# Two attention blocks on one core: A's x and first query weights are loaded from ScalarE's queue

## The chip, the cores and the metric

The kernel runs on one core of a Trainium2 chip. TensorE multiplies matrices, VectorE and ScalarE work elementwise, GpSimd does small set-up work, and SyncE (SP) computes nothing: it issues loads and stores. All loads and stores are carried out by 16 DMA engines. The metric is the device time of one launch in microseconds (us); lower is better.

## The reference

Two independent attention blocks with a key and value cache are computed, and their outputs are set side by side. All data is bf16; the batch is 16, there are 32 queries for each batch element and a cache of 1024 keys, heads have 128 elements, and the model width is 1024.

```python
q = (x @ wq).reshape(B, Sq, 32, 128).transpose(0, 2, 1, 3)
scores = einsum("bhqd,bhkd->bhqk", q, k) * 128 ** -0.5
o = einsum("bhqk,bhkd->bhqd", softmax(scores), v)
out = o.transpose(0, 2, 1, 3).reshape(B, Sq, 32 * 128) @ wo
```

Block A has 4 key and value heads that 8 query heads share each; block B has 32 key and value heads. The caches of B are 128 MB each and those of A 16 MB each, and the kernel reads every byte once, about 338 million bytes in all.

## The kernel before

The kernel streams the caches through SBUF and interleaves A's and B's work. In the code the index `pi` is 0 for A and 1 for B. B's K tiles go through 8 buffers (`KB_sb`), its V tiles through 6 (`VB_sb`), A's through two of each (`KA_sb`, `VA_sb`). A step computes scores on TensorE, the row maximum on VectorE (L1038), the exponential on ScalarE (L1051), transposes of the probabilities on TensorE, and the product with V on TensorE (L1083 for A, L1116 for B). B's K is transposed in place on VectorE (L976), A's on TensorE (L969). The output projection (L823) follows each group.

The first 40 us are a prologue. `xT_stage` (L655) loads x in four pieces of 0.25 MB for each block (L659; `x1_0` to `x1_3` for B, `x0_0` to `x0_3` for A), transposes each piece with eight TensorE transposes (L671), and copies the result to `xT_sb` on ScalarE or VectorE (L651). The pieces 1 to 3 of a block are declared to read what its piece 0 writes, so their issue waits for piece 0 to land. `wq_load` (L707) loads query weights in four pieces of 0.5 MB (L714): `wq0` to `wq3` into `wq_sb`, except for A's first part, which goes into `woA_sb` as `wqA0` to `wqA3`. Then TensorE projects the queries, L754 for B and L735 for A.

The program is not emitted in the order in which it is written. Each operation is recorded with an engine, what it reads and writes, and, for a load, a semaphore key (`dma_key`). `list_schedule` (L249) simulates all engines with the durations of a table, gives each operation a start time `t0`, and chooses ScalarE or VectorE for operations that either can do. The operations are then sorted by `t0` into one list (L494) and recorded again, which derives the dependences and waits anew. `emit_all` (L507) gives each engine its own operations in the order of that list. So the order on an engine is fixed when the program is built, and an instruction that waits holds back everything behind it on its engine.

All loads are recorded for SP. They are issued in list order into one queue: `x1_0`, `x0_0`, `wq0` to `wq3`, `wqA0`, A's first K tile, `x1_1` to `x1_3`, `x0_1` to `x0_3`, `wqA1` to `wqA3`, and then B's K and V tiles and the rest. Seven of the eight output rows that are stored from `acc` go through GpSimd's queue (L847).

Of the kernel before, what the change touches and what calls it, by code (L numbers as in the profile page):

```python
# [23 lines left out]
WQ_DELAY = 1  # L24
A_STEPS_FRAC = 0.96
SP_STRICT = False
SP_AHEAD = 5
DMA_MARGIN = {"kb_dma": 0.5, "vb_dma": 0.5, "ka_dma": 0.5, "va_dma": 0.5}
DMA_MARGIN_DEFAULT = 2.0
# [88 lines left out]
def actual(res):  # L118
    out = []
    for r in res:  # L120
        if not isinstance(r, Virt):
            out.append(r)
        else:
            out.append((r.cls, r.idx))
    return tuple(out)


class Prog:
# [120 lines left out]
    def list_schedule(self, lat=0.05, look=LOOK):  # L249
        ops = self.ops  # L250
        n = len(ops)
# [133 lines left out]
        order = []  # L385
# [34 lines left out]
        while True:  # L420
# [7 lines left out]
            for eng, lst in ready.items():  # L428
# [3 lines left out]
                if eng == "sp":  # L432
                    fe = max(fe, dma_free[0] - SP_AHEAD)
                if eng == "dve":
# [17 lines left out]
                key = (st, end, -bl[ci])  # L452
# [12 lines left out]
            if beng == "sp":  # L465
                st = max(st, dma_free[0] - SP_AHEAD)
            if beng == "pe":
# [23 lines left out]
                if ndeps[u] == 0:  # L491
                    make_ready(u)
        assert len(order) == n, "cycle in dependency graph?"
        seq = sorted(range(n), key=lambda k: (ops[order[k]].t0, k))  # L494
        newp = Prog()
        for k in seq:
            eng, emit, reads, writes, dma_key, name, dur, tag, prio = self.specs[order[k]]
            if eng == "any":
                eng = chosen[order[k]]
                name = name + "@" + eng  # L500
            newp.add(eng, emit, actual(reads), actual(writes), dma_key, name, dur, tag, prio)
        return newp

# [899 lines left out]
```

## Time and profile before

| What | Value |
|---|---|
| median of 3 runs | 850.99 us (847.71 to 854.19) |
| the profiled execution | 851.34 us, its span 849.5 us |
| granted TensorE clock, mean | 0.995 |
| TensorE busy | 783.0 us (92%) |
| VectorE busy | 727.0 us (86%) |
| ScalarE busy | 623.6 us (73%) |
| SP's queue | 337.95 million bytes |
| DMA rate over the span | 402 GB/s |

The span is the part of an execution that the profile covers, from the first instruction to the last. Busy times are sums over the span and not over stages: an engine with 92% can still be the one that everything waits for in one stage and idle in another. In the page's slices a digit is the busy share in tenths, and 9 means 90% or more. L numbers are lines of the kernel before.

### The profile page before, as it was taken

Reading aid. Unit: us, or ns where it says so; the run is one execution under the profiler, and the core shown is the slowest. Engines: PE = TensorE matmul, PEld = TensorE weight load, DVE = VectorE, ACT = ScalarE, POOL = GpSimd, SP = SyncE. Lnnn points to the kernel's source line nnn. Section 1 sums busy time; section 2 is a strip of 40 time slices with the busy share of each in tenths; the row PEclk is TensorE's granted clock in tenths of the full one; section 3 lists DMA queues with packets and bytes.
Section 4 is the critical chain, followed back from the end, with each engine's and each line's share of the span. In section 5 each row is a group of like instructions: output and inputs, shape, how many; then the busy total and the mean of one; then the engine's idle time right before and its main releaser. Section 6 shows DMA issues by size and latency. Waiting matters only on the chain.

```text
span 849.5 us, 29749 instructions
## 1 busy us (share of the span) xinstructions
PE 783.0 (92%) x13056; PEld 522.6 (62%) x13056; DVE 727.0 (86%) x1018; ACT 623.6 (73%) x1363; POOL 6.1 (1%) x20
## 2 busy tenths in 40 slices
PE   7989999999898999998999988999899998899878
PEld 4456665666565566665666665666666666666655
DVE  1499987979799898987999898998999978998995
ACT  3497787778677777786788787677877867686874
POOL 1000000000000000000000000000000000000000
PEclk9999999999999999999999999999999999999999
DMA  9999999999999999999999999999999999999995
GB/s 339 415 412 414 411 411 410 405 393 394 416 384 412 409 395 415 416 398 412 414 392 408 411 392 416 415 416 405 410 402 415 412 414 415 415 400 414 416 418 226
DMA packets 112208, 341.68 MB, mean 402 GB/s; under 512 B 12048, under 2 KB 12304, under 8 KB 112080
## 3 DMA queue, kind: packets, MB, share of 16 engines
q1 hardware_dynamic: 111520, 337.95, 100.0%
q8 instruction: 103, 1.69, 0.7%
q0 software_dynamic: 560, 1.84, 0.5%
q14 instruction: 25, 0.20, 0.1%
HBM read 337.64 MB, written 2.10 MB: 400 GB/s over the span
## 4 chain that ended last, share of the span: by engine, by line
PE 55%; DVE 23%; ACT 14%; DMA 5%; issue 2%; SPq 1%; DVEq 0%; ACTq 0%
DVE stat L1038 10%; PE psum L1116 10%; PE psum L823 10%; DVE KB_sb L976 8%; ACT P_sb L1051 8%; PE psum L1027 6%; PE psum L1063 5%; PE psum L754 5%; PE psum L1097 5%; PE psum L1083 4%; DMA KB_sb<-in_B_k_cache_dram 4%; PE psum L995 4%; PE psum L735 4%; ACT PT_sb L651 2%; ACT O_sb L1174 1%
## 5 line engine op out<-in xcount | busy, mean ns | idle before, releaser
L1038 DVE TENSOR_REDUCE stat<-psum 128x1 f32<-128x1024 f32 x256 | 303.6, 1210 | 50.7 <-PE psum L995 31.5
L1051 ACT ACTIVATE P_sb<-psum,stat 128x1024 bf16<-128x1024 f32 x246 | 275.9, 1122 | 63.2 <-DVE stat L1038 59.7
L976 DVE STREAM_TRANSPOSE KB_sb<-KB_sb 128x1024 f32<-128x1024 f32 x240 | 286.6, 1222 | 6.2 <-DMA KB_sb<-in_B_k_cache_dram 6.0
L651 ACT COPY PT_sb<-psum 128x512 f32<-128x512 f32 x226 | 131.4, 604 | 35.2 <-PE psum L1063 22.0
L1116 PE MATMUL psum<-VB_sb,PT_sb 64*64 64x256 bf16 x3584 | 116.2, 271 | 8.6 <-ACT P_sb L1051 5.2
L1116 PEld LDWEIGHTS psum<-VB_sb,PT_sb 64*64 64x64 bf16 x3584 | 97.0, 107 | 27.7 <-issue 25.5
L1174 ACT ACTIVATE O_sb<-psum,stat 128x128 bf16<-128x128 f32 (+1 forms) x205 | 80.8, 417 | 43.2 <-PE psum L1083 23.1
L1063 PE MATMUL psum<-id,P_sb 128*128 128x128 f32 x512 | 88.7, 297 | 6.9 <-ACT P_sb L1051 4.1
L1063 PEld LDWEIGHTS psum<-id,P_sb 128*128 128x128 f32 x512 | 74.0, 208 | 25.2 <-ACT P_sb L1051 13.8
L995 PE MATMUL psum<-KTA_sb,QT_sb 128*128 128x512 bf16 x256 | 84.4, 384 | 3.1 <-ACT P_sb L1051 1.6
L1083 PE MATMUL psum<-VA_sb,PT_sb 128*128 128x128 bf16 x1024 | 78.8, 221 | 7.5 <-ACT P_sb L1051 2.6
L1083 PEld LDWEIGHTS psum<-VA_sb,PT_sb 128*128 128x128 bf16 x1024 | 63.2, 99 | 31.6 <-issue 12.0
L1027 PE MATMUL psum<-KB_sb,QR 32*32 32x512 bf16 x3840 | 73.3, 394 | 8.1 <-ACT P_sb L1051 4.6
L1097 PE MATMUL psum<-id,P_sb 128*128 128x128 f32 x472 | 76.2, 287 | 4.1 <-ACT P_sb L1051 3.5
L754 PE MATMUL psum<-wq_sb,xT_sb 128*128 128x512 bf16 x256 | 72.4, 394 | 3.3 <-DMA wq_sb<-in_B_wq_dram 1.6
L1097 PEld LDWEIGHTS psum<-id,P_sb 128*128 128x128 f32 x472 | 63.8, 193 | 17.3 <-ACT P_sb L1051 7.5
L823 PE MATMUL psum<-woB_sb,OTB_sb 128*128 128x512 bf16 x256 | 66.9, 380 | 2.4 <-ACT P_sb L1051 1.7
L1027 PEld LDWEIGHTS psum<-KB_sb,QR 32*32 32x32 bf16 x3840 | 43.8, 89 | 35.3 <-ACT P_sb L1051 8.3
L823 PE MATMUL psum<-woA_sb,OTA_sb 128*128 128x512 bf16 x256 | 62.8, 380 | 0.4 <-ACT OTA_sb L651 0.3
L735 PE MATMUL psum<-xT_sb,wq_sb 128*128 128x512 bf16 x192 | 54.2, 380 | 1.7 <-issue 1.2
L1051 ACT ACTIVATION_READ_ACCUMULATOR P_sb<-psum,stat 128x1 f32 x246 | 50.3, 205 | 0.0
L835 DVE TENSOR_TENSOR acc<-acc,psum 128x512 f32<-128x512 f32 x64 | 41.3, 675 | 9.6 <-PE psum L823 9.4
(74 smaller groups left out, 720.2 us busy)
## 6 DMA issues: line engine op xcount, KB each, us to landing
KB_sb<-in_B_k_cache_dram SPq DMA_DIRECT2D x240, 512.0 KB, 8.9
VB_sb<-in_B_v_cache_dram SPq DMA_DIRECT2D x234, 512.0 KB, 7.8
KA_sb<-in_A_k_cache_dram SPq DMA_DIRECT2D x64, 256.0 KB, 7.8
VA_sb<-in_A_v_cache_dram SPq DMA_DIRECT2D x64, 256.0 KB, 8.0
wq_sb<-in_B_wq_dram SPq DMA_DIRECT2D x16, 512.0 KB, 8.3
woB_sb<-in_B_wo_dram SPq DMA_DIRECT2D x32, 256.0 KB, 8.5
woA_sb<-in_A_wo_dram SPq DMA_DIRECT2D x32, 256.0 KB, 7.0
wq_sb<-in_B_k_cache_dram SPq DMA_DIRECT2D x16, 512.0 KB, 11.5
```

The costliest lines, as they stand in the source:

```text
L651: return e.copy(dst, src) if hasattr(e, "activation") else e.tensor_copy(dst, src)
L754: last = e.matmul(bank(v)[:, 0:CW], xT_sb[:, 1, j, G * P:(G + 1) * P], wq_sb[:, j, mh * CW:(mh + 1) * CW], start=(j == 0), stop=(j == DJ - 1))
L823: last = e.matmul(bank(v)[:, 0:OUTW], OT[:, gp, hh, :], wo_[:, hh, oh * OUTW:(oh + 1) * OUTW], start=(hh == 0), stop=(hh == nh - 1))
L976: pr.add("dve", lambda e: e.transpose(tile_k(x).bitcast(F32), tile_k(x).bitcast(F32)), writes=[home_k(x)], name="KBt_tr", rtag={home_k(x): ...
L995: pr.add("pe", lambda e, u=u: e.matmul(bank(vS[u]), qt[:, q.b, q.hh0:q.hh0 + 4, :].rearrange("p a q -> p (a q)"), KTA_sb[:, sl, u * 512:(u ...
L1027: last = e.matmul(bank(q.vS[g2])[32 * x:32 * x + 32, :].rearrange("p (s j) -> p s j", s=16), lhsT, rhs, start=(fp == 0), stop=(fp == 3), t ...
L1038: pr.add("dve", lambda e: e.tensor_reduce(stat[:, vst.idx, 0:1], both(vS), AXIS.XY, ALU.max, negate=True), writes=vS + [vst], name="max")
L1051: return e.activation(dst, src, ACTF.Exp, bias=stat[:, vst.idx, 0:1], scale=1.0, accum_out=stat[:, vst.idx, 1:2])
L1063: last = e.transpose(bank(vb)[:, m * P:(m + 1) * P], p32[:, m:Sk // 2:NPK], id32[:])
L1083: last = e.matmul(bank(vb)[:, 0:Dh], ptc_of(vPT, c, 0, P), VA_sb[:, kvs, c, :], start=(c == 0), stop=(c == NCH - 1))
L1097: last = e.transpose(bank(vb)[:, m * P:(m + 1) * P], p32[:, 4 * h + m:Sk:8], id32[:])
L1116: last = e.matmul(bank(q.vbo)[n0:n0 + 64, 0:2 * Dh].rearrange("p (i d) -> p i d", i=2), pt2_chunk(vPT, c, e0, n0), v2[e0:e0 + 64, :, c, :] ...
```

## The change

Loads whose key starts with `x0` or `wqA` are sorted to the front of the list and recorded for ScalarE instead of SP. There are eight: `x0_0` to `x0_3` and `wqA0` to `wqA3`, 3.0 MB in all. Among themselves they keep the order of the list: `x0_0`, `wqA0`, `x0_1` to `x0_3`, `wqA1` to `wqA3`. ScalarE issues them ahead of its first copy, into its own queue. All other operations keep their engine and their order. The schedule itself is not simulated anew.

```diff
+ON_ACT = ('x0', 'wqA')
...
-        seq = sorted(range(n), key=lambda k: (ops[order[k]].t0, k))
+        seq = sorted(range(n), key=lambda k: (-1.0 if str(ops[order[k]].dma_key).startswith(ON_ACT) else ops[order[k]].t0, k))
         newp = Prog()
         for k in seq:
             eng, emit, reads, writes, dma_key, name, dur, tag, prio = self.specs[order[k]]
             if eng == "any":
                 eng = chosen[order[k]]
                 name = name + "@" + eng
+            if dma_key is not None and dma_key.startswith(ON_ACT):
+                eng = "act"
             newp.add(eng, emit, actual(reads), actual(writes), dma_key, name, dur, tag, prio)
```

## The prediction, made before the result was known

> **What bounds the kernel now.** I read the page first, then the start of the timeline, the chain of work, the tables by stage, and last the landings of single loads. (MB is 1024 x 1024 bytes here; x1 and wq are B's x and query weights, x0 and wqA are A's.) The page gives the chain by engine and the DMA engines' load:
>
> ```profile
> PE 55%; DVE 23%; ACT 14%; DMA 5%; issue 2%; SPq 1%; DVEq 0%; ACTq 0%
> DMA  9999999999999999999999999999999999999995
> ```
>
> The reader is to see two limits lying on each other: the DMA engines are full to the last slice, and yet the chain that ends last runs nearly all of its length through computing. The stages tell which one gives way:
>
> ```profile
> 4.00:6.00 2.00, 1.54 (x15) 1.28 (x13) 0.00 (x0) 1.28 (x2) 0.00 (x0) 1.00 0.89 220
> 190.00:200.00 10.00, 9.86 (x143) 5.96 (x139) 9.68 (x11) 8.77 (x19) 0.00 (x0) 1.00 0.98 359
> ```
>
> The last number is GB/s. Most stages have 400 to 418; 190 to 200 has 359, 240 to 250 has 354, 430 to 440 has 373. There the loads had run short because buffers came free late, so computing sets the pace at those points. In return, data is late to the engines by only 1.0 us in all after 50 us (VectorE's waits for KB loads, 0.2, 0.5 and 0.3 us). So a shift of all computing in the first 40 us should reach the end nearly whole, and the question is what the change does to those 40 us.
>
> The timeline of the start (start, duration, engine, line):
>
> ```profile
> 0.74 1.28 ACT L651 ACT_TABLE_LOAD   x1 [0.74 <-PEq L1388]
> 0.74 0.38 SPq L659 DMA_DIRECT2D acc<-in_B_x_dram  x1
> 1.17 0.42 SPq L659 DMA_DIRECT2D acc<-in_A_x_dram  x1
> 1.65 1.96 SPq L714 DMA_DIRECT2D wq_sb<-in_B_wq_dram  x4
> 4.72 1.93 ACT L651 COPY xT_sb<-psum 128x1024 bf16<-128x1024 bf16 x2 [2.70 <-PE psum L671]
> 7.61 1.43 SPq L659 DMA_DIRECT2D acc<-in_A_x_dram  x3
> 9.08 1.46 SPq L714 DMA_DIRECT2D woA_sb<-in_A_wq_dram  x3
> ```
>
> and the chain there and at its next DMA link:
>
> ```profile
> 1.65 5.44 DMA wq_sb<-in_B_wq_dram
> 7.13 5.79 PE psum L754 x14
> 18.93 6.22 PE psum L735 x28
> 25.51 12.86 DMA KB_sb<-in_B_k_cache_dram
> ...
> 198.67 10.08 DMA KB_sb<-in_B_k_cache_dram
> ```
>
> TensorE starts B's projection (L754) the moment wq's first quarter has landed, and is then busy without a gap over 0.5 us until 38 us. Each load here has its own semaphore, and the trace has the moment of its last arrival: x1_0 3.56, x0_0 4.14, wq 7.08, 8.41, 9.69 and 10.94, wqA0 12.23, A's first K 12.92, x1_1 to x1_3 13.55, 14.17 and 14.81, x0_1 to x0_3 until 16.75, wqA1 to wqA3 until 20.64. They land strictly in the order of issue. From wq0 on (1.0 MB in) each 0.5 MB takes 1.27 us, so a landing is 7.08 + 2.55 us for each MB beyond the first. The tile's row agrees (wq0 issued at 1.65, wq3 at 3.14, the two ends of it):
>
> ```profile
> DMA to landing us min/median/max: 5.4/6.7/7.8
> ```
>
> **The change part by part.** *Removed from SP:* eight issues, 0.42 + 1.10 + 1.43 + 1.46 = 4.4 us. SP is not on the path there: wq's first issue comes 0.47 us earlier, but its landing is set by bytes ahead of it. Later issues on SP (K and V of B) come up to 4.4 us earlier into a queue that is full anyway; worth nothing while computing is late.
>
> *Added to ScalarE, ahead of its first copy:* x0_0, wqA0, x0_1 to x0_3, wqA1 to wqA3. L660 makes x0_1 depend on x0_0, and in the trace the issue of x0_1 carries that wait. On SP at 7.61 us it was long met; on ScalarE it is the third instruction and stands until about 4.15 us, with every copy of ScalarE behind it. Then six issues at SP's spacing (0.475 us for x, 0.49 for wq) are 2.9 us, to 7.1. The table load (1.28 us) belongs to the first copy (its line is L651), so I place it behind the issues: 8.4; if it stays ahead of them, the six begin at about 4.9 instead and the copy starts 0.7 us sooner, which the next step swallows. The first copy (1.01 us) ends at 9.4 where it ended at 5.7. Cover was 1.4 us (5.7 against the landing of wq0 at 7.08); gone, TensorE starts 2.3 us late.
>
> *The price of an issue on ScalarE* is not in this trace. Ends: 0.05 us (an event row on TensorE) and 2.06 us (the longest issue on SP near the start, into a full queue); I take SP's 0.475, the same instruction into a queue that isn't full.
>
> *Moved loads and those that they pass:* all of A's 3.0 MB now stand in a second queue beside SP's x1_0, wq, K and x1_1 to x1_3 (3.25 MB). What B's first work needs was ahead of most of A's; now they compete. How two load queues share is not in this trace. The nearest row is an output from GpSimd's queue beside SP's (690.3 to 692.8 us; packets, MB, share):
>
> ```profile
> q1 hardware_dynamic: 227, 0.79, 77.5%
> q0 software_dynamic: 79, 0.26, 25.4%
> ```
>
> The second queue didn't stand behind SP's backlog; it took a quarter of the bytes at once. Ends: the second queue gets between a quarter and a half. I take the half, because both queues now hold the same kind of load (2 KB rows) and many of them, where the output was one transfer of 64 rows.
>
> With halves, SP's item that ends at s MB lands when 2s MB are through: wq0 (0.75) 8.4, wq1 10.9, wq2 13.5, wq3 (2.25) 16.0, K 17.3, x1_1 18.6, x1_2 19.8, and x1_3 when all 6.25 MB are through, 20.5 by the formula and 20.64 by the present landing of wqA3, which is the same byte. B's sixteen matmuls (two projections, four matmuls a quarter, 1.6 us) end at 16.0 + 1.6 = 17.6 instead of 13.3: +4.3. Then come the transposes in TensorE's fixed order x1_1, x1_2, x1_3, x0_1, x0_2, x0_3. A's x is long there but stands behind x1_3: 20.6 + four times 0.55 = 22.8, the last ScalarE copies end at 23.7, and A's projection (L735) starts at about 23.8 instead of 18.93: **+4.8**. With a quarter, SP's 3.25 MB need 4.3 MB in all, x1_3 lands at 15.6, and ScalarE's +2.3 to +2.5 remains.
>
> From there TensorE is full until 38 us, and the shift passes to the first scores (36.24) and VectorE's first max (36.88). VectorE's next step waited 0.29 us for K, landing at 38.37 after 12.9 us in a full queue, the same byte count as before; so 0.3 us are absorbed: **+4.5**. Behind 42 us the chain has no DMA link until 198.67. Downstream waits for data could take back at most 1.0 us.
>
> *Sum:* the profiled execution took 851.34 us (span 849.5), the median is 850.99. 850.99 + 4.5 = 855.5.
>
> **A rule of the Trainium skill.** The page DMA: Bandwidth & Descriptors ("Queues, rings and completion order") says that a DMA engine takes turns between the queues that have work, a packet at a time. By it the share is near a half and the time 855.5; by the output's row alone, 853.4. The same page ("Issuing engines are not separate DMA queues") says that issuing from a second engine saves only the issuing time. The trace agrees as far as it goes: SP issued wq in 1.96 us and the bytes landed until 10.94.
>
> **The rivals.**
> *ScalarE's stall alone, +2.4: 853.4.* The two queues are served in order of issue, or SP keeps three quarters. For it: 77.5% in the output's row. Against it: that was another kind of transfer.
> *Nothing arrives at the end: 851.0.* The shift is taken up by waits for data. For it: full DMA engines. Against it: 1.0 us of such waits, and the short stages at 190, 240 and 430 us, where loads wait for computing. This is also what a change without effect would give.
> *Dear issues on ScalarE: 857 to 863.* At 1.10 us each (wqA0's issue now) ScalarE's copy ends at 13.1, B's projections at 19.3, +6.0: 857. At 2.06 they end at 25.1, +11.8 less 0.3: 862.5. It decides over the shares from about 0.9 us an issue. SP's own issues slow to 1.10, 0.85 and 0.7 us between 3.65 and 6.4 us, the very time when ScalarE would issue.
> *Faster: 849.6.* Between 4 and 6 us only 220 GB/s move, with SP's queue full. If a second queue fills that hole (0.38 MB short, 1 us), ScalarE's copies stay under wq0's landing, and wq0 lands 0.47 us sooner with its issue, the shift is -1.4. It needs six issues in under 0.6 us after x0_0's landing (0.1 each) and a small share for A's queue: SP's row has 0.43 to 0.47.
>
> **How the numbers follow.** Halves 0.50 (855.5), stall alone 0.20 (853.4), nothing 0.11 (851.0), dear issues 0.10 (857 to 862.5), faster 0.09 (849.6). The runs shown spread from 847.71 to 854.19, so under 1% (8.5 us) is about what a measurement here can't tell from no change. The range reaches from the faster case to most of the dear one, 849.5 to 860.5. Slower by over 1% (above 859.5) needs issues above 1.5 us: 0.08; faster by over 1% has no mechanism above: 0.02; within: 0.90.
>
> **What would show it.** Right: eight issues on ScalarE, the third standing until about 4.2 us; its first copy starting near 8.4; wq3 landing near 16; x1_3 near 20.6; L735 starting near 23.8; all of A's loads landed before x1_3; the first max 4 to 5 us later; more slices of DMA below 400 GB/s between 45 and 65 us. Wrong: wq landings unmoved (no sharing), L735 within 3 us of 18.93, or a first max that is late with an end that is not.

## The result and the profile after

The changed kernel takes 854.52 us in the median of 20 runs, the kernel before 851.65 us beside it: a ratio of **1.0044 (95% interval 1.0028 to 1.0060)**, or +3.7 us (2.4 to 5.1). The forecast was +4.5 us. A second measurement gave 1.0048 (1.0029 to 1.0067). The profiled execution took 853.13 us (span 851.2).

The page of the changed kernel, the lines that answer to those shown of before, and the queues:

```profile
PE 57%; DVE 22%; ACT 14%; DMA 5%; issue 2%; SPq 0%; DVEq 0%; ACTq 0%
DMA  9999999999999999999999999999999999999995
q1 hardware_dynamic: 109856, 334.81, 98.8%
q10 hardware_dynamic: 1664, 3.15, 1.0%
```

The shape of the whole is unchanged. New is q10, ScalarE's queue, with 3.15 million bytes, which are the eight loads. Its start in the timeline (start, duration, engine, line; ACTq is ScalarE's issuing):

```profile
0.74 0.41 ACTq L662 DMA_DIRECT2D acc<-in_A_x_dram  x1
1.18 2.09 SPq L717 DMA_DIRECT2D wq_sb<-in_B_wq_dram  x4
1.18 0.46 ACTq L717 DMA_DIRECT2D woA_sb<-in_A_wq_dram  x1
4.53 1.62 ACTq L662 DMA_DIRECT2D acc<-in_A_x_dram  x3
6.19 1.69 ACTq L717 DMA_DIRECT2D woA_sb<-in_A_wq_dram  x3
7.90 1.28 ACT L654 ACT_TABLE_LOAD   x1 [7.90 <-issue]
9.20 1.93 ACT L654 COPY xT_sb<-psum 128x1024 bf16<-128x1024 bf16 x2
10.35 6.56 PE L757 MATMUL psum<-wq_sb,xT_sb 128*128 128x512 bf16 x16 [4.04 <-ACT xT_sb L654]
```

ScalarE stands from 1.64 to 4.53 us, issues until 7.87, loads its table, and starts its first copy at 9.20 us instead of 4.72. TensorE's first projection waits 4.04 us for that copy and starts at 10.35 instead of 7.13. The chain of the changed kernel's first 45 us then takes another way (start, duration, what):

```profile
5.25 14.21 DMA acc<-in_B_x_dram
...
19.50 1.22 PE psum L674 x16
...
22.77 7.07 PE psum L738 x32
...
44.57 1.18 PE psum L1030 x35
45.78 2.36 DVE stat L1041 x2
```

The load that ends late is x1_3, B's last piece of x: issued at 5.25, landed at 19.45, where before it landed at 14.81. A's projection (L738, the L735 of before) starts at 22.77 instead of 18.93, **+3.84 us**, the first scores at 40.1 instead of 36.24, and the second row maximum at 45.78 instead of 42.04. So the whole loss is there by 23 us, and at 200 us it is still there: TensorE's weight loads, taken one by one in order, are 3.7 us late against the first profile of before.

Two causes ran side by side in the forecast: ScalarE's **stall**, and the **sharing** of the DMA engines by two queues. The profile shows both, and can't tell which of them the time is lost by. That is what the experiments are for.

### The profile page after: what moved, and what is told of

Same layout as the page of the kernel before. It is cut to its first block, busy times and chain, and to the rows that moved or that the text cites. A ratio compares the mean times of both kernels' runs of the same rounds, so it can differ in the third digit from the quotient of the medians.

```text
span 851.2 us, 29749 instructions
## 1 busy us (share of the span) xinstructions
PE 782.0 (92%) x13056; PEld 522.4 (61%) x13056; DVE 725.4 (85%) x1018; ACT 623.0 (73%) x1363; POOL 6.1 (1%) x20
## 3 DMA queue, kind: packets, MB, share of 16 engines
q10 hardware_dynamic: 1664, 3.15, 1.0%
## 4 chain that ended last, share of the span: by engine, by line
PE 57%; DVE 22%; ACT 14%; DMA 5%; issue 2%; SPq 0%; DVEq 0%; ACTq 0%
DVE stat L1041 11%; PE psum L1119 10%; PE psum L826 9%; ACT P_sb L1054 8%; DVE KB_sb L979 8%; PE psum L1030 6%; PE psum L1066 5%; PE psum L757 5%; PE psum L1100 5%; PE psum L738 5%; PE psum L998 4%; PE psum L1086 4%; DMA acc<-in_B_x_dram 2%; ACT PT_sb L654 2%; DMA KB_sb<-in_B_k_cache_dram 2%
## 5 line engine op out<-in xcount | busy, mean ns | idle before, releaser
L738 PE MATMUL psum<-xT_sb,wq_sb 128*128 128x512 bf16 x192 | 54.2, 380 | 1.6 <-issue 1.1
```

## The experiments

Times are ratios to the kernel before, measured beside it, with 95% intervals. The moments of this table are from the profiles (us from the start of the span): ScalarE's first copy, the first projection of B, the landing of x1_3, the first projection of A, the first scores.

| Kernel | copy | B's proj. | x1_3 | A's proj. | scores | ratio |
|---|---|---|---|---|---|---|
| before | 4.72 | 7.13 | 14.81 | 18.93 | 36.24 | |
| before, again | 4.55 | 7.98 | 16.05 | 20.16 | 37.47 | 1.0013 (1.0000 to 1.0027) |
| changed | 9.20 | 10.35 | 19.45 | 22.77 | 40.08 | 1.0044 (1.0028 to 1.0060) |
| changed, again | 9.01 | 10.17 | 19.70 | 23.02 | 40.33 | 1.0048 (1.0029 to 1.0067) |
| stall alone | 10.48 | 11.64 | 15.87 | 22.51 | 39.82 | 1.0034 (1.0020 to 1.0049) |
| stall that took no hold | 4.69 | 6.32 | 15.57 | 19.25 | 36.56 | 0.9991 (0.9975 to 1.0007) |
| six loads behind the copies | 5.47 | 7.51 | 17.77 | 22.29 | 39.60 | 1.0068 (1.0043 to 1.0093) |
| no wait for x0_0 | 6.43 | 7.77 | 20.45 | 23.75 | 41.06 | 1.0077 (1.0047 to 1.0106) |
| stall doubled | 15.01 | 16.17 | 16.86 | 28.00 | 45.31 | 1.0064 (1.0045 to 1.0083) |
| stall doubled, again | 12.95 | 14.11 | 14.81 | 26.15 | 43.46 | 1.0088 (1.0067 to 1.0108) |
| A's weights only | 4.93 | 9.81 | 18.31 | 23.02 | 40.33 | 1.0043 (1.0023 to 1.0062) |
| A's x only | 6.95 | 8.11 | 16.31 | 19.95 | 37.26 | 1.0015 (0.9994 to 1.0035) |
| B's first quarter on ScalarE | 4.86 | 6.74 | 13.81 | 17.46 | 34.77 | 0.9962 (0.9946 to 0.9978) |
| the same, again | 4.76 | 6.55 | 14.51 | 18.16 | 35.47 | 0.9982 (0.9967 to 0.9996) |

Two profiles of the same kernel before differ by 1.2 us in the first scores, so differences under about that are not read from one profile.

**The stall alone.** All loads stay on SP; only the first copy waits in addition for B's third weight quarter.

```diff
+            if name.startswith("xT_ev") and not held_back:
+                held_back = True
+                reads = tuple(reads) + (("wq", 2),)
             newp.add(eng, emit, actual(reads), actual(writes), dma_key, name, dur, tag, prio)
```

> All loads stay on SP in the old order; only ScalarE's first copy waits in addition for the third quarter of B's query weights, which lands at 9.69 us in the kernel before. Stall theory (ScalarE's late first copy is enough by itself, and a shift of the prologue passes whole to the end): first copy at 9.7 instead of 4.72, L754's projections from about 10.85 instead of 7.13, A's projection from about 22.7 instead of 18.93, the time +3.5 us. Sharing theory (B's loads, slowed by A's bytes in a second queue, are what costs): the copies were covered, the time 0 to +1 us.

Measured: 1.0034, +2.9 us (1.7 to 4.2), and 3.0 us later at the first scores than the mean of the two profiles of before (36.86). The timeline, and then the chain:

```profile
10.48 1.93 ACT L655 COPY xT_sb<-psum 128x1024 bf16<-128x1024 bf16 x2 [4.57 <-DMA wq_sb<-in_B_wq_dram]
11.64 5.28 PE L758 MATMUL psum<-wq_sb,xT_sb 128*128 128x512 bf16 x16 [6.24 <-ACT xT_sb L655]
```

```profile
22.51 7.07 PE psum L739 x32
```

A stall is enough by itself: with no second queue at all, a late copy puts A's projection at 22.51, nearly as late as the changed kernel's (22.77). But this stall is not of the changed kernel's size. The copy starts 1.3 us later than there (10.48 against 9.20), and the sixteen projections behind it made that good, in 5.28 us instead of 6.56, because they came to their fast spacing after 3.4 us instead of 5.9 (last section). A stall of the changed kernel's own size was not tried alone.

**A longer stall.** The same edit with A's first K tile in place of the weight quarter.

> As the run before, but the first copy waits for A's first K tile (12.92 us): the stall of the first projection is 7.0 us instead of 3.7. If shifts pass whole: +6.7 us, and 3.2 more than the shorter stall. If later waits for data take shifts up: the second step of 3.3 us comes out clearly below 3, or both below their shift by the same 1 to 2 us.

Measured: 0.9991 (0.9975 to 1.0007), and the first copy at 4.69. The copy didn't wait: in the sorted list the copy stands ahead of the K load, so it doesn't depend on it; instead the load waits for the copy and is issued at 5.73 instead of 4.79. It says nothing of a stall, but serves as a control: one load held up by 1 us on SP, with those behind it, costs nothing that this measurement can see. The edit was then made with the K load recorded just ahead of the first copy:

```diff
+        copy0 = min(op.t0 for op in ops if op.name.startswith("xT_ev"))
+        seq = sorted(range(n), key=lambda k: (min(ops[order[k]].t0, copy0 - 1e-6) if ops[order[k]].dma_key in ("wqA0", "ka0") and ops[order[k]].t0 < 10.0 else ops[order[k]].t0, k))
...
+                reads = tuple(reads) + (("KA", 0),)
```

> The longer stall as it was meant: A's first K tile is recorded just ahead of the first copy (SP's order unchanged), so the first copy does wait for its landing, 12.92 to 13.9 us. The first projection starts near 14.2 (+7.0), A's projection near 25.9 (+7.0), the first max 7 us late. If a shift passes whole: +6.7 us, twice the shorter stall. If later waits for data or run-short stages take some up: +4 to +5.

> The double stall again: the first time the prologue was 9.0 us late and the time only +5.4 us (1.0045 to 1.0083), while the short stall gave 3.5 late and +2.9. If a large shift is partly taken up, the time is again +4 to +6.5 us, clearly below the shift in the prologue, and the profile shows where the shift shrinks; if the first time was chance, +8 to +9.

Measured: +5.4 us (3.8 to 7.1), and again +7.5 us (5.7 to 9.2), with first scores 8.5 and 6.6 us late. Twice the stall costs about twice as much. The two means are 6.5 and 7.5 us: most of a large shift reaches the end, and whether a part of it is taken up isn't settled. In the second profile, weight load by weight load against the second profile of before, the lag is 6.0 us at 51 us and still 5.7 at 226; it falls to 2.6 by 254 us because TensorE stood still there in the profile of before and not in this one (last section), and is 4.7 at the end.

**Sharing without the stall: six loads behind the copies.** The last six of A's loads are issued behind ScalarE's first two copies.

```diff
+        behind = sorted(op.t0 for op in ops if op.name.startswith("xT_ev"))[1] + 1e-6
+        seq = sorted(range(n), key=lambda k: ((-1.0 if ops[order[k]].dma_key in ("x0_0", "wqA0") else behind) if str(ops[order[k]].dma_key).startswith(ON_ACT) else ops[order[k]].t0, k))
```

> The eight loads are on ScalarE's queue, but the last six are issued behind its first two copies, so that no copy waits for an issue. Sharing theory: first projection near 7.6, but the queues share from about 9 us, x1_3 lands near 18.3 instead of 14.81, A's projection starts near 21.5 (+2.6), the time +2.4 us. Stall theory: without the stall the first projection is +0.5 at most and the time within +0.5 us of before.

Measured: 1.0068, +5.8 us (3.7 to 7.9). The first copy is 0.8 us late (5.47), the first projection 0.4 us, and still A's projection is 3.4 us late. x1_3 lands at 17.77, 3.0 us later than in the first profile of before, and the 32 transposes behind it run at half clock and take 3.60 us; the same 32 take 2.28 us in the changed kernel. So about 1.3 of the 3.4 us belong to the clock in this profile, and the rest is near the 2.6 us expected. The chain, then the timeline, and last the 32 transposes of the changed kernel:

```profile
5.27 12.50 DMA acc<-in_B_x_dram
21.45 0.70 DVE xT_sb L655
22.29 7.07 PE psum L739 x32
```

```profile
7.51 4.56 PE L758 MATMUL psum<-wq_sb,xT_sb 128*128 128x512 bf16 x12 [1.22 <-DMA wq_sb<-in_B_wq_dram]
17.82 3.60 PE L675 MATMUL psum<-ident,acc 128*128 128x128 bf16 x32 [0.63 <-DMA acc<-in_B_x_dram]
```

```profile
19.50 2.28 PE L674 MATMUL psum<-ident,acc 128*128 128x128 bf16 x32 [0.54 <-DMA acc<-in_B_x_dram]
```

Sharing is enough by itself, too, but the time is well above the 2.4 us expected, and more than this kernel's first scores are late (2.7 us against the mean of before). In this profile TensorE ran twice at half clock in the first 125 us (the column ahead of the DMA share is the granted clock), which neither profile of before did; seven runs are too few to tell how often that happens.

```profile
18.00:21.40 3.40, 3.40 (x33) 3.36 (x33) 0.69 (x1) 1.89 (x3) 0.00 (x0) 0.50 1.03 415
120.40:123.80 3.40, 3.40 (x28) 1.55 (x27) 2.30 (x2) 2.28 (x4) 0.00 (x0) 0.50 1.03 410
```

Such an early stretch is in two more profiles, that of the next kernel (from 14.9 us on) and the second of the changed kernel (from 120.8, where its lag behind the second profile of before grew from 2.8 to 5.7 us), and in none of the six in which SP alone issued. Whether loads on ScalarE's queue bring such stretches on more often was not tested; it may be a part of these kernels' loss.

**Sharing without the wait.** In the changed kernel, x0_1 to x0_3 no longer depend on x0_0.

```diff
             if dma_key is not None and dma_key.startswith(ON_ACT):
                 eng = "act"
+                if dma_key in ("x0_1", "x0_2", "x0_3"):
+                    reads = ()
```

> The changed kernel, but x0_1 to x0_3 no longer wait for x0_0, so ScalarE issues all eight back to back, to about 4.9 us; table load, copies from 6.2, first projection near 8. Both queues are full from the start. Sharing theory: x1_3 still last, 19.5 to 20.5, A's projection at 22.8 to 23.5, the time as in the changed kernel, +3.8 to +4.3. Stall theory: +0.5 to +1 us.

Measured: 1.0077, +6.5 us (4.0 to 9.0). The first copy comes at 6.43 and the first projection at 7.77, yet x1_3 lands at 20.45 and A's projection starts at 23.75. To take the wait away doesn't help; it fills A's queue sooner, and B's loads are later still. Here too the time is above the lateness of the first scores (4.2 us), though its interval reaches down to it.

**One group at a time.** Only A's weights are moved, and in another kernel, with `('x0',)`, only A's x.

```diff
-ON_ACT = ('x0', 'wqA')
+ON_ACT = ('wqA',)
```

> Only A's four weight loads go to ScalarE's queue; none of them waits, so ScalarE has issued them by 2.7 us, the table is loaded by 4.0, and no copy is late. Sharing theory: B's weights compete from the start, wq0 lands near 9 instead of 7.08 and wq3 near 15, x1_3 near 18; A's projection 3 to 4 us late, the time +3 to +4 us. Stall theory: 0 to +0.5 us.

> Only A's four pieces of x go to ScalarE's queue: three of them wait for the first, are issued from 4.2 to 5.7 us, then the table, first copy near 7.0 instead of 4.72, first projection near 8.1 (+1.0). 1 MB competes, wq3 lands near 12.5 and x1_3 near 16. Both theories: A's projection +1.0 to +1.5, the time +1 to +1.5 us. If moving the loads cost something by itself (a fixed price of a second queue), it would be as large as for all eight, +3.8.

Measured: the weights alone 1.0043, +3.7 us (2.0 to 5.3), the whole loss of the change; x alone 1.0015, +1.3 us (-0.5 to 3.0). With the weights alone no instruction of ScalarE waits for a load and the first copy is at 4.93, but B's projection waits for B's own weights (timeline):

```profile
9.81 1.89 PE L757 MATMUL psum<-wq_sb,xT_sb 128*128 128x512 bf16 x4 [2.74 <-DMA wq_sb<-in_B_wq_dram]
12.39 1.04 PE L757 MATMUL psum<-wq_sb,xT_sb 128*128 128x512 bf16 x2 [0.69 <-DMA wq_sb<-in_B_wq_dram]
```

A fixed price of a second queue as large as the whole loss is ruled out: x alone, with four issues, one wait and 1 MB, has A's projection 1.0 us late and costs 3.0 us at most.

**The queue used for what is needed first.** In the kernel before, B's first weight quarter alone is issued by ScalarE.

```diff
+        early = [k for k in range(n) if ops[order[k]].dma_key in ("wq0",) and ops[order[k]].t0 < 10.0]
+        seq = sorted(range(n), key=lambda k: (-1.0 if k in early else ops[order[k]].t0, k))
...
+            if k in early:
+                eng = "act"
```

> The kernel before with one load moved: B's first weight quarter is issued on ScalarE's queue at 0.74 us, beside x1_0 on SP's; nothing else moves. No instruction waits on ScalarE for it. It competes with x1_0 and x0_0 only (1.0 MB as before), but the two queues should fill the hole in the transfers between 4 and 6 us: wq0 lands near 6.5 instead of 7.08, the first projection 0.5 us earlier, the time -0.5 us, too little to be told from no change by times; the landings tell it.

> B's first weight quarter alone on ScalarE's queue, again. If the first result (0.9962) came from its landing at 5.2 instead of 7.1 us, the landing and A's projection (17.5 instead of 18.9) repeat, and the time is -1.5 to -3 us. If it was chance, 0 to -1 us and a projection that is earlier all the same.

Measured: 0.9962, -3.2 us (-4.6 to -1.9), and again 0.9982, -1.5 us (-2.8 to -0.3). **This kernel beats both.** The first lead is clearly above the 0.5 us expected, the second interval still holds 0.5. The quarter lands at 5.18 and 4.93 us instead of 7.08 and 7.93, and A's projection starts at 17.46 and 18.16 instead of 18.93 and 20.16. A part of the quarter's lead is that it passes x0_0, which now lands at 5.83 and 5.63 instead of 4.14 and 4.11. TensorE transposes x0_0 ahead of its first projection, so it waits for x0_0 and no longer for the quarter (timeline of the first profile):

```profile
5.87 1.07 PE L675 MATMUL psum<-ident,acc 128*128 128x128 bf16 x8 [1.04 <-DMA acc<-in_A_x_dram]
6.74 4.57 PE L758 MATMUL psum<-wq_sb,xT_sb 128*128 128x512 bf16 x16
```

Between 4 and 6 us (last column GB/s; first the kernel before in its second profile, then this one):

```profile
4.00:6.00 2.00, 1.37 (x13) 1.12 (x11) 0.00 (x0) 1.45 (x2) 0.00 (x0) 1.00 0.91 294
```

```profile
4.00:6.00 2.00, 0.95 (x10) 0.71 (x9) 0.00 (x0) 1.01 (x1) 0.00 (x0) 1.00 1.05 399
```

The hole in the transfers is filled (in the second profile to 347 GB/s), and the loads behind it land sooner: A's first K tile, on which the chain of both profiles goes on, at 11.87 and 12.65 us instead of 12.92 and 14.16. About 1 us of the lead in the first profile is luck in TensorE's speed (last section).

**The two kernels again.**

> The kernel before against itself, for the spread and a second profile. Its ratio is 1 within its interval. In the first profile TensorE stood 2.2 us for no visible cause within one L1116 group at 228 us and ran 3.4 us at half clock behind it. If that is chance, it may be gone or elsewhere in this profile; if it belongs to this kernel's timing, it is there again.

> The changed kernel again, on the chip and beside the runs of the three others of this call: A's projection starts 3.5 to 4 us later than in the kernel before, the time +3 to +4.5 us (first measurement 1.0044).

Measured: the kernel before against itself 1.0013 (1.0000 to 1.0027), so an interval here can miss 1 by a hair without a cause; the changed kernel 1.0048, +4.1 us (2.5 to 5.7).

## Why the prediction was right, step by step

**The whole.** The way, +4.5 us against +3.7 measured, and both mechanisms held. The "nothing arrives" and "faster" rivals fell, and so did "stall alone" as an account of the mechanism: its +2.4 us lies at the edge of the measured interval, but the two queues shared by halves (below), and the run with A's weights alone, without a stall, cost as much.

**The stall was sized too small.** Forecast: x0_0 lands about 4.15, six issues at 0.475 us, first copy at 8.4, TensorE +2.3. Measured: x0_0 landed at 4.51, with SP's loads beside it; the six issues took 3.37 us from 4.53, 0.56 each; first copy at 9.20, TensorE +3.2. The table load stood behind the issues, as placed. The miss doesn't show in the sum, because the later of the two delays decides and that was the sharing.

**The sharing was sized too large.** Forecast with halves: wq3 at 16.0, x1_3 at 20.6, A's projection at 23.8, +4.8. Measured: 14.14, 19.45 and 22.77, +3.84. Two reasons show in the rows. One is A's queue: x0_1 was issued only at 4.53, and A's queue ran nearly dry. From 7 to 8.5 us (packets, MB, share):

```profile
q1 hardware_dynamic: 253, 0.49, 89.3%
q10 hardware_dynamic: 54, 0.09, 16.0%
```

The forecast had both queues full from the first moment on. Of the 0.58 MB here, A's queue had 0.2 MB less than half; so its last load, wqA3, landed at 21.73, behind x1_3, where the forecast had all of A's loads land ahead of it. The other is the hole between 4 and 6 us, which the forecast kept and which the second queue filled for the most part (353 GB/s instead of 220, 0.27 MB in 2 us). An estimate from these rows, at 400 GB/s: 0.5 and 0.7 us, about the 1.15 us by which x1_3 was forecast too late.

```profile
4.00:6.00 2.00, 1.61 (x15) 1.62 (x16) 0.00 (x0) 0.00 (x0) 0.00 (x0) 1.00 1.03 353
```

**They don't add, and each is enough.** The forecast had the stall as the smaller part, +2.3, that sharing raises to +4.8. In the changed kernel the stall alone has B's transposes begin 3.6 us late (17.65 instead of 14.07), and the late x1_3 adds only TensorE's idle 0.54 us ahead of 19.50. How much the stall is worth there depends on the slow matmuls: they took 6.56 us for the sixteen projections, where the kernel before took 6.20 and the second profile 5.96, and in that profile the waits for x1_2 and x1_3 add 0.59 and 0.64 us. The runs show the same from outside: stall without sharing 1.0034, sharing without stall 1.0043 to 1.0077. The cost is near that of the later of the two, not of their sum.

**The share of two queues.** The half was right where both had work. From 12 to 17 us, and from 18.5 to 20, when SP's queue had come to B's K with 4 KB rows:

```profile
q10 hardware_dynamic: 543, 1.05, 54.2%
q1 hardware_dynamic: 540, 0.98, 51.1%
```

```profile
q1 hardware_dynamic: 115, 0.40, 64.9%
q10 hardware_dynamic: 112, 0.23, 39.2%
```

The packets are nearly equal both times; in the second stretch the bytes are not, because SP's rows are twice as long. The rule of the Trainium skill that I weighed (DMA: Bandwidth & Descriptors, "Queues, rings and completion order": engines take turns between queues packet by packet) agrees with that. The other one, that a second engine saves only issuing time ("Issuing engines are not separate DMA queues"), looks too narrow for this start. With wq0 on ScalarE's queue the last of the first three loads was issued 0.48 us sooner (1.17 instead of 1.65), and all three (x1_0, x0_0 and wq0, 1.0 MB) had landed at 5.83 and 5.63 us, where the six profiles with SP alone have 6.27 to 8.65. The nearest two are only 0.44 us apart, so this rests on the two groups not overlapping.

**Absorbed, 0.3 us.** Not so: the second maximum waited for TensorE's scores (0.42 us) and not for K any more, and was 3.74 us late, as the scores of A were 3.84.

**Passed whole to the end.** Held for the change: +3.84 in the prologue (+3.2 and +3.5 in the first scores of its two profiles against the mean of before), +3.7 and +4.1 in the times. The profiled pair alone would mislead, 853.13 against 851.34: it lost 2.1 us of its lag on the way, at places where the first profile of before had delays of its own, such as 3.4 us at half clock from 705 us on. Against the second profile of before, the lag is 2.6 us at 51 us and 2.6 at 717; at the end it is 1.6, since both profiles have 3.4 us at half clock in between, at 801 and at 826 us.

**Dear issues.** 0.56 us, not 1.10: that rival didn't come, though the direction of its doubt was right.

**The other signs.** The first maximum was 3.85 us late (40.73), a little under the 4 to 5 named. The short stages came: from 40 to 60 us the changed kernel's four stretches of 5 us have 331, 297, 318 and 357 GB/s, before 405, 418, 404 and 422. SP's loads waited longer there for buffers that TensorE frees (A's K tiles 9.6 us instead of 3.8), so computing sets the pace, as the forecast had it.

## What to carry to other kernels

Where the DMA engines are already busy (401 GB/s from 7 to 15 us with two queues here, 406 with one), a second queue doesn't add bandwidth: it re-orders, and what it moves forward pushes something else back. Ask which bytes the next instruction waits for, and put those, and only those, into it. An engine that computes pays for every issue and every wait of a load in its own stream (0.56 us an issue and 2.9 us of standing here), and two such costs that lie in parallel hide each other, so that removing one shows nothing. Here nearly all of a delay in the first 20 us was seen in the time, but only over many runs; single profiles lose or gain as much on the way.

## What was not expected of the hardware

**A hole in the first transfers.** With SP's queue alone the rate between 4 and 6 us is 220 to 304 GB/s in six profiles, though the queue had work (in the first of before, 2.5 MB issued by 3.6 us, 0.5 MB landed by 4.14); with loads on ScalarE's queue from the start it is 316 to 399. B's first K tile, behind the same 6.25 MB in nearly all kernels, landed at 21.86, 23.10, 22.93, 22.62, 23.91 and 21.86 us in the six profiles in which SP alone issued, and at 20.86 to 21.65 in the seven with a second queue where it stands behind the same bytes. What makes the hole wasn't tried.

**TensorE's first matmuls.** The sixteen matmuls of B's first projections start 0.43 us apart and take 634 ns each, until at some moment they take 380 and start 0.22 apart. That moment came 1.7 us after the first of them in the first profile of the kernel with wq0 on ScalarE, 3.8 in its second, and 5.1 and 5.9 us in the two of before, while the granted clock reads 1.00. In that kernel's first profile B's projections ended at 11.3 us and its chain goes on with A's K tile, landing at 11.87; with the 6.20 us that the kernel before needed for them they would have ended near 12.9, so about 1 us of its lead is chance. The Trainium skill (TensorE: Matmul & The Clock Gate, "Part 1: The HAM clock gate") states that after idling the array runs at half clock for a window whose phase is free, 427 ns apart instead of 216; the trace agrees with the two spacings, but the slow stretch lasted from 1.7 to 5.9 us in these profiles, and with A's weights alone on ScalarE's queue all sixteen were slow, over 7.2 us with their waits for loads, where it gives about 3.4.

**A standstill that comes and goes.** In 9 of the 14 profiles TensorE stands 2.2 to 2.5 us in the middle of one group of B's product with V, with no releaser. First the two profiles of before, then that of the kernel with wq0 on ScalarE, which ran through:

```profile
226.58 1.62 PE L1116 MATMUL psum<-VB_sb,PT_sb 64*64 64x256 bf16 x52
230.42 0.52 PE L1116 MATMUL psum<-VB_sb,PT_sb 64*64 64x256 bf16 x12 [2.22 <-issue]
```

```profile
230.90 0.52 PE L1116 MATMUL psum<-VB_sb,PT_sb 64*64 64x256 bf16 x12 [2.25 <-issue]
```

```profile
224.44 1.94 PE L1120 MATMUL psum<-VB_sb,PT_sb 64*64 64x256 bf16 x64
```

In the first profile of before the 16 KB packet of the instruction queue (q8) that follows the one of 217.65 us starts at 228.22, 10.6 us later, and TensorE goes on at 230.42; in the profile that ran through, the packets start at 215.70, 222.92 and 229.04. In all nine profiles with the standstill two of these packets are 10.4 to 10.7 us apart there, and TensorE goes on 2.2 to 2.5 us after the late one; in the other five they are 7.2 to 7.4 us apart. So it looks like instructions that came late; why they are late was not tested. In the first profile of before, 3.4 us at half clock follow from 230.8. The second profile of the kernel with wq0 had the standstill and its first had not, so it isn't fixed by the kernel. Between two single profiles this is worth about 3 us, nearly the effect of the change.
